# Putting the y stage of an attention and two-layer feed-forward kernel into the planner's one order

## The chip, the cores and the metric

The kernel runs on one core of a Trainium2 chip. The metric is device time in microseconds (us) of one execution, as the median of several runs. The engines are TensorE (PE), VectorE (DVE), ScalarE (ACT), GpSimd (POOL) and SyncE (SP, which issues most DMAs). Each works through its own list of instructions in order.

## The reference

Three layers follow each other; the second uses x = attention output (2304 tokens, 512 wide), the third uses y.

```python
# attention: B=4, H=8, S=576, D=64, causal softmax, plus a memory read-out, mixed by sigmoid(beta)
x = (g * mem_out + (1 - g) * local)          # -> [2304, 512]
# layer 2: w_in [512, 2048], w_out [2048, 512]
r = np.maximum(x @ w_in, 0.0)
y = (s * (r * r) + b) @ w_out
# layer 3: w_gate, w_val [512, 1536], w_out2 [1536, 512]
out = (1 / (1 + np.exp(-(y @ w_gate))) * (y @ w_val)) @ w_out2
```

## The kernel before, in words

Every large product is taken in two terms: an operand is split into a rounded high part and the low rest, and PE adds hi times hi, lo times hi and hi times lo. So each product step is 12 matmuls: 3 terms by 4 blocks of 128.

**Attention** works on 16 jobs, each two heads of one batch. When the four jobs of a batch are done, their sum XB is split into x (`s_hi` on ACT, L885; `s_lo`, L889, on the engine that `ENG["split"]` names, here DVE), in two windows of 256 and 320 tokens. **h** takes 128 chunks, 8 such windows by 16 blocks `f` of w_in (L316); ACT applies the relu (L326), and SP stores pairs of chunks to the scratch tensor `r_d` (L330). **The y stage** goes over 5 windows of tokens (256, then four of 512) by 16 blocks f, 80 steps in all; I call them y0 to y4. A step loads r back (`load_r`, L977), squares it on ACT (L1030), scales and shifts it on DVE (L1031), rounds the high part gh on ACT (L1035), takes the low part gl on DVE in even steps and on POOL in odd ones (L1037), and runs 12 matmuls with the block of w_out (L1053). After a window, `y_out` splits the sums on ACT and DVE (L1007) and stores the first three windows (L1013). **The gv stage** (L1124, L1094) then does layer 3.

**Weights** lie in memory as 64-bit words. `load_weight` (L219) loads a block of 512 KB into a raw buffer of the pool `stage` (two buffers; L228, L232), then scales on ACT (L242), shifts and joins on DVE (L245, L248, L254), rounds the high part on ACT (L260) and takes the low part on POOL (L263), which releases the raw buffer.

**The order.** `Plan` (L36) is a list scheduler: each task has an engine, a cost in ns, an urgency (the smaller, the sooner), what it reads, and slots that it needs; `plan.order()` gives one order for all engines, and the program is issued in it under `tc.manual_schedule()` (L958). `TUNE` holds the urgencies. Only the attention, the w_in loads and h are in the plan. The y stage stands behind it (from `att.close()`, L961), written as a plain loop with `load_gv` at every third step; there the framework's scheduler decides. Pools that reuse attention memory open when the last instruction on that memory is done.

```python
    with tc.manual_schedule():
        for n in plan.order():
            plan.tasks[n][2]()
    att.close()
```

Of the kernel before, what the change touches and what calls it, by code (L numbers as in the profile page):

```python
# [20 lines left out]
FB = 1  # L21
RATE = 160.0

TUNE = {
# [3 lines left out]
    "relu": -5000.0,  # L28
}
ENG = {"split": "DVE"}  # L30
RR = 4
LEAD = 1
DEFER = 3
# [112 lines left out]
def attention_moe_kernel(  # L146
# [72 lines left out]
    def load_weight(pool, src, name, cols, pieces=None):  # L219
# [204 lines left out]
    def stack_lo(t, ds):  # L424
# [9 lines left out]
        "PTC": 1, "XB": 1, "x0": 1, f"x{SPLIT}": 1, "raw": 2, "f": FB, "w": 1, "wt": 16,  # L434
# [14 lines left out]
    def plan_load(j):  # L449
# [454 lines left out]

    def plan_h(m):
        b, c0, n, f = chunks[m]
        u = AT["h"] + m * AT["hs"]
        add(
# [15 lines left out]

    def plan_w_in(f):
        u = AT["w"] + f * AT["ws"]

        def pieces(load, scaled, rest, joined, high, low):
            def last():
                w_in_sb[f] = low()  # L930

            add("SP", 600, load, u + AT["lw"], new=[("raw", ("raw", f)), ("wt", ("wt", f))], late=1900, size=5e5)
            add("ACT", 670, scaled, u, reads=[("raw", f)], new=[("f", ("f", f))])
            add("DVE", 1400, rest, u, writes=[("raw", f)])
            add("DVE", 800, joined, u, reads=[("f", f)], writes=[("raw", f)])
            add("ACT", 660, high, u, reads=[("raw", f)], writes=[("wt", f)])
            add("POOL", 1360, last, u, reads=[("raw", f)], writes=[("wt", f)])

        load_weight(w1, w_in[:, f * P : (f + 1) * P], f"w_in{f}", True, pieces)
# [21 lines left out]
    att.close()  # L961


    w2 = ctx.enter_context(tc.tile_pool(name="w2", bufs=19, side="right"))
    wins = [(max(0, i), 512 + min(i, 0)) for i in range(-NT % 512 and NT % 512 - 512, NT, 512)]
    w_out_sb = {}
    gp = ExitStack()
    gpool = gp.enter_context(tc.tile_pool(name="gp", bufs=2, side="right"))
    steps = [(wi, f) for wi in range(len(wins)) for f in range(NF)]
    r_sb = {}  # L970

    def load_r(n):
# [22 lines left out]
    ps_yb = gp.enter_context(tc.tile_pool(name="ps_yb", bufs=4, space=PSUM))
    ybuf = {}
    kept = 2
    ngv = 0
    ydone = []

    def y_out():
        wi, acc = ydone.pop()
        c0, n = wins[wi]
        yt = yp.tile([P, 2, NK, 512], F32R, tag="y", name=f"ya{wi}")
        for d in range(NK):
            nc.scalar.copy(yt[:, 0, d, :n], acc[d][:, :n])
            nc.vector.tensor_tensor(  # L1007
                out=yt[:, 1, d, :n], in0=acc[d][:, :n], in1=yt[:, 0, d, :n].bitcast(F32),
                op=ALU.subtract,
            )  # L1010
        if wi < len(wins) - kept:
            for x, dst in enumerate((yh_d, yl_d)):
                nc.sync.dma_start(  # L1013
                    dst[:, c0 : c0 + n].rearrange("(c p) n -> p c n", p=P),
                    yt[:, x, :, :n].bitcast(F32),
                )
        else:
# [166 lines left out]
```

## Time and profile before

| what | us |
|---|---|
| median of 3 runs | 1155.8 (1155.66 to 1156.09) |
| the profiled execution | 1153.03 |
| its span, first to last instruction | 1151.0 |
| busy in the span: PE / DVE / ACT / POOL | 1082.7 / 601.5 / 541.1 / 332.5 |

The mean clock granted to TensorE is 0.98 of full speed. The profiled execution is 2.8 us under the median of the runs, and 2.0 us of it lie outside the span. Read the profile by stage: attention with h to some 472 us, y to 699 us, gv to the end; each has another limit.

### The profile page before, as it was taken

Reading aid. Unit: us, or ns where it says so; the run is one execution under the profiler, and the core shown is the slowest. Engines: PE = TensorE matmul, PEld = TensorE weight load, DVE = VectorE, ACT = ScalarE, POOL = GpSimd, SP = SyncE. Lnnn points to the kernel's source line nnn. Section 1 sums busy time; section 2 is a strip of 40 time slices with the busy share of each in tenths; the row PEclk is TensorE's granted clock in tenths of the full one; section 3 lists DMA queues with packets and bytes.
Section 4 is the critical chain, followed back from the end, with each engine's and each line's share of the span. In section 5 each row is a group of like instructions: output and inputs, shape, how many; then the busy total and the mean of one; then the engine's idle time right before and its main releaser. Section 6 shows DMA issues by size and latency. Waiting matters only on the chain.

```text
span 1151.0 us, 16974 instructions
## 1 busy us (share of the span) xinstructions
PE 1082.7 (94%) x6232; PEld 932.8 (81%) x6232; DVE 601.5 (52%) x1178; ACT 541.1 (47%) x1176; POOL 332.5 (29%) x363
## 2 busy tenths in 40 slices
PE   4787999999999998998899989999999999999998
PEld 3665998999999998876678867888888888888897
DVE  5988879776766745688864587311211111111122
ACT  5768877777777754566545555211111111111121
POOL 5646656443354223444432353000000000000000
PEclk9778999999999999999999999999999999999999
DMA  5333454332322157676645454002000200100000
GB/s 118 90 92 83 137 147 133 95 104 83 86 81 74 47 164 208 198 225 192 219 141 180 133 169 120 9 0 73 37 1 7 104 1 1 37 37 1 1 38 19
DMA packets 128290, 105.96 MB, mean 92 GB/s; under 512 B 67024, under 2 KB 110032, under 8 KB 128208
## 3 DMA queue, kind: packets, MB, share of 16 engines
q1 hardware_dynamic: 125616, 100.17, 29.4%
q10 hardware_dynamic: 2592, 4.72, 1.1%
q8 instruction: 49, 0.80, 0.3%
q14 instruction: 33, 0.27, 0.1%
HBM read 76.03 MB, written 28.84 MB: 91 GB/s over the span
## 4 chain that ended last, share of the span: by engine, by line
PE 71%; DVE 10%; DMA 8%; POOL 4%; ACT 3%; issue 3%; SPq 0%; DVEq 0%; POOLq 0%; ACTq 0%
PE gv L1124 25%; PE oa L1094 13%; PE h L316 12%; PE y L1053 7%; DMA raw_w_out<-in_moe_w_out_dram 4%; PE sc L620 3%; PE acc L800 2%; PE acc L801 2%; DMA raw_gv<-in_moe_w_val_dram 2%; POOL P L678 2%; PE pt_B L747 2%; DMA raw_gv<-in_moe_w_gate_dram 1%; POOL w_out L263 1%; PE sc L646 1%; PE acc L804 1%
## 5 line engine op out<-in xcount | busy, mean ns | idle before, releaser
L316 PE MATMUL h<-x,w_in 128*128 128x256 f32 (+1 forms) x1536 | 230.4, 302 | 6.7 <-ACT r L326 5.6
L316 PEld LDWEIGHTS h<-x,w_in 128*128 128x128 f32 x1536 | 208.8, 190 | 16.0 <-ACT r L326 9.9
L1133 DVE TENSOR_TENSOR sg<-gv,sg 128x512 f32<-128x512 f32 (+1 forms) x60 | 38.2, 637 | 300.5 <-PE gv L1124 300.5
L1124 PE MATMUL gv<-yb,gv 128*128 128x512 f32 (+1 forms) x864 | 172.4, 355 | 0.0
L1053 PE MATMUL y<-gh,w_out 128*128 128x512 f32 (+1 forms) x640 | 148.8, 375 | 17.3 <-ACT gh L1035 17.2
L1124 PEld LDWEIGHTS gv<-yb,gv 128*128 128x128 f32 x864 | 143.9, 188 | 25.2
L1053 PEld LDWEIGHTS y<-gh,w_out 128*128 128x128 f32 x640 | 112.0, 189 | 44.7 <-ACT gh L1035 25.1
L1094 PE MATMUL oa<-w_out,ph 128*128 128x512 f32 x432 | 143.7, 392 | 0.0
L1124 PE MATMUL gv<-ya,gv 128*128 128x512 f32 x576 | 136.2, 392 | 0.1
L1124 PEld LDWEIGHTS gv<-ya,gv 128*128 128x128 f32 x576 | 108.0, 188 | 24.6 <-ACT sg L1131 0.5
L1131 ACT ACTIVATE sg<-gv 128x512 f32<-128x512 f32 (+1 forms) x60 | 33.3, 555 | 195.6 <-PE gv L1124 195.4
L1135 ACT CAST ph<-sg 128x512 fp32r<-128x512 f32 (+1 forms) x60 | 34.6, 577 | 146.4 <-DVE sg L1133 146.4
L678 POOL TENSOR_SCALAR P<-P,rs 128x384 f32<-128x384 f32 (+4 forms) x144 | 86.3, 623 | 41.2 <-DVE rs L674 32.9
L1094 PEld LDWEIGHTS oa<-w_out,ph 128*128 128x128 f32 x432 | 81.1, 188 | 17.8
L662 ACT ACTIVATE P<-P,nm 128x384 f32<-128x384 f32 (+2 forms) x144 | 83.7, 583 | 13.4 <-DVE nm L600 12.3
L1094 PE MATMUL oa<-w_out,pl 128*128 128x512 f32 x216 | 84.5, 391 | 0.0
L600 DVE CUSTOM_DVE_ANT_0 P<-sc,mask 128x384 f32<-128x384 f32 (+2 forms) x144 | 70.3, 514 | 24.2 <-PE sc L620 14.9
L1053 PE MATMUL y<-gl,w_out 128*128 128x512 f32 (+1 forms) x320 | 80.3, 373 | 2.5 <-POOL gl L1037 1.5
L1031 DVE TENSOR_SCALAR rr<-rr,sb_s,sb_b 128x512 f32<-128x512 f32 (+1 forms) x80 | 55.2, 697 | 45.7 <-ACT rr L1030 45.4
L1037 POOL TENSOR_TENSOR gl<-rr,gh 128x512 fp32r<-128x512 f32 (+1 forms) x40 | 52.4, 1309 | 76.3 <-ACT gh L1035 60.4
L326 ACT ACTIVATE r<-h 128x320 f32<-128x320 f32 (+1 forms) x128 | 52.4, 409 | 45.3 <-PE h L316 38.5
L1030 ACT ACTIVATE rr<-rr 128x512 f32<-128x512 f32 (+1 forms) x80 | 46.6, 588 | 51.2 <-DMA rr<-relu_scratch 50.7
(118 smaller groups left out, 1648.5 us busy)
## 6 DMA issues: line engine op xcount, KB each, us to landing
rr<-relu_scratch SPq DMA_DIRECT2D x64, 256.0 KB, 3.1
raw_w_out<-in_moe_w_out_dram SPq DMA_DIRECT2D x28, 512.0 KB, 3.6
relu_scratch<-r SPq DMA_DIRECT2D x32, 320.0 KB, 2.2
raw_w_in<-in_moe_w_in_dram SPq DMA_DIRECT2D x16, 512.0 KB, 4.1
relu_scratch<-r SPq DMA_DIRECT2D x32, 256.0 KB, 2.5
raw_gv<-in_moe_w_gate_dram SPq DMA_DIRECT2D x12, 512.0 KB, 3.7
raw_gv<-in_moe_w_val_dram SPq DMA_DIRECT2D x12, 512.0 KB, 3.8
out_dram<-o ACTq DMA_DIRECT2D x18, 256.0 KB, 2.0
```

The costliest lines, as they stand in the source:

```text
L316: nc.tensor.matmul(t[:, :n], wt[:, wi, c], x[:, xi, c], start=(m == 0), stop=(m == 3 * NK - 1))
L326: nc.scalar.activation(rts[b, c0, f - f % 2][:, f % 2, :n], t[:, :n], AF.Relu)
L600: nc.vector.tensor_tensor_reduce(out=pr, in0=ps, in1=mk, scale=1.0, scalar=3e38, op0=ALU.add, op1=ALU.min, accum_out=nm,)
L662: nc.scalar.activation(pr, pr, AF.Exp, bias=T.pop(("nm", j, e, t)), scale=-1.0, accum_out=T["sums", j][:, col : col + 1],)
L678: nc.gpsimd.tensor_scalar(out=pr, in0=pr, scalar1=T["rs", j, part][:, n : n + 1], scalar2=1.0, op0=ALU.mult, op1=ALU.mult,)
L1030: nc.scalar.activation(r, r, AF.Square)
L1031: nc.vector.tensor_scalar(out=r, in0=r, scalar1=sb_s, scalar2=sb_b, op0=ALU.mult, op1=ALU.add)
L1037: (nc.vector, nc.gpsimd)[step % 2].tensor_tensor(out=gl, in0=r, in1=gh.bitcast(F32), op=ALU.subtract)
L1053: nc.tensor.matmul(acc[d][:, :n], w_out_sb[f][:, x, d], y, start=(f == 0 and x == 0 and y is gh), stop=(f == NF - 1 and y is gl),)
L1094: nc.tensor.matmul(acc[tt], a[:, ts], w_out2_sb[f][:, x].rearrange("p c f -> p (c f)"), start=(f == 0 and a is ph and x == 0), stop=(f == ...
L1124: nc.tensor.matmul(t[:, :n], wt[:, a, c], yt[:, x, c, :n], start=(m == 0), stop=(m == 3 * NK - 1),)
L1133: nc.vector.tensor_tensor(out=pf[:, :n], in0=ps[1][:, :n], in1=sg[:, :n], op=ALU.mult)
```

## The change

- All tasks of the y stage enter the plan: the 16 w_out blocks (`plan_w_out`), the first 16 of the 24 w_gate and w_val blocks (`plan_gv`), the steps (`plan_step`) and the window ends (`plan_y_out`). Two tasks of no engine open the pools: `open_y`, when all attention tasks are issued ("bar1"), and `open_yp`, when all h tasks are too ("bar2"). y0 needs only the first, so its steps may stand between the last h chunks; y1 to y4 need the second.
- The late weights get raw buffers of their own, three instead of two ("raw2"). The pool w2 has 16 buffers instead of 19, so three of the twelve w_out2 blocks more wait for the end of the y stage (w3 has 4 instead of 1).
- `ENG["split"]` goes from DVE to POOL.
- y is stored by block d, 8 DMAs of up to 256 KB in a window, instead of 2 of up to 1 MB.
- The planner's costs, its DMA rate and every number in `TUNE` are set anew, so the attention's order moves too. The last 8 blocks of w_gate and w_val, all of w_out2 and the gv stage stay outside the plan.

```diff
-RATE = 160.0
+RATE = 250.0
...
-    "relu": -5000.0,
+    "relu": -5000.0, "wo": 29802.5, "wos": 17.7, "gv": 39611.4, "gvs": 94.4, "y": 13878.2,
+    "lead": -44.8, "lr": -193.8, "ys": -70.4, "yss": -0.0,
 }
-ENG = {"split": "DVE"}
+ENG = {"split": "POOL"}
 RR = 4
-LEAD = 1
-DEFER = 3
...
+        "raw2": 3, "f2": FB, "w2": 16, "rr": RR, "gh": 3, "gl": 3, "yacc": 2, "yt": 2,
...
+    def plan_weight(pool, src, name, cols, u, key, tag, done, ins=(), late=False):
+        raw = "raw2" if late else "raw"
...
+            add(
+                "SP", 450, load, u + AT["lw"], reads=ins,
+                new=[(raw, ("raw", key)), (tag, key)], late=1900, size=5e5,
+            )
+            f = "f2" if late else "f"
+            add("ACT", 670, scaled, u, reads=[("raw", key)], new=[(f, ("f", key))])
+            add("DVE", 1500, rest, u, writes=[("raw", key)])
+            add("DVE", 850, joined, u, reads=[("f", key)], writes=[("raw", key)])
+            add("ACT", 660, high, u, reads=[("raw", key)], writes=[key])
+            add("POOL", 1360, last, u, reads=[("raw", key)], writes=[key])
...
+    def open_y():
+        att.close()
+        Y["w2"] = ctx.enter_context(tc.tile_pool(name="w2", bufs=16, side="right"))
+        Y["gp"] = gp.enter_context(tc.tile_pool(name="gp", bufs=2, side="right"))
+        Y["stage"] = gp.enter_context(tc.tile_pool(name="stage2", bufs=3, side="right"))
+        Y["ps", 0] = gp.enter_context(tc.tile_pool(name="ps_ya", bufs=4, space=PSUM, side="right"))
...
+        add(
+            "PE", 12 * mm(n), y_mm, u,
+            reads=[gk, ("gl", step), ("wo", f)] + (["bar2"] if wi else ["bar1"])
+            + ([("yc", step - 1)] if step else []),
+            writes=[("yc", step)] + ([] if new else [("ya", wi)]), new=new, late=250,
+        )
...
+        def store(d):
+            nc.sync.dma_start(yh_d[d * P : (d + 1) * P, c0 : c0 + n], box["t"][:, 0, d, :n].bitcast(F32))
+            nc.sync.dma_start(yl_d[d * P : (d + 1) * P, c0 : c0 + n], box["t"][:, 1, d, :n].bitcast(F32))
...
+    for key, opened, before in (("bar1", open_y, bar1), ("bar2", open_yp, h_parts)):
+        n = add("BAR", 0, opened, 0, reads=["bar1"] if key == "bar2" else [], writes=[key], late=0)
+        plan.tasks[n][4].update(before)
...
-    w2 = ctx.enter_context(tc.tile_pool(name="w2", bufs=19, side="right"))
...
-            if ngv < 19 and f % 3 == 0:
-                load_gv(ngv)
-                ngv += 1
...
+        for f in range(8)
     ]
     gp.close()
-    w3 = ctx.enter_context(tc.tile_pool(name="w3", bufs=1, side="right"))
+    w3 = ctx.enter_context(tc.tile_pool(name="w3", bufs=NF2 - 8, side="right"))
```

Three places show how instructions move. In the names, h_3_256_12 is the chunk of batch 3, window from token 256, block f = 12; y0_2 is the sum of window y0 in output block 2; gh0_1, gl0_1 and rr0_1 are window 0, step 1; gv3_1 is block 3 of w_val (gv3_0: of w_gate). x12 counts alike matmuls.

**PE, where h ends and y0 starts.** Before:

```order
L316 MATMUL h_3_256_12_6187<-x3_256_5777,w_in12_2050 128x320 x12
L316 MATMUL h_3_256_13_6203<-x3_256_5777,w_in13_2193 128x320 x12
L316 MATMUL h_3_256_14_6217<-x3_256_5777,w_in14_2434 128x320 x12
L316 MATMUL h_3_256_15_6233<-x3_256_5777,w_in15_2512 128x320 x12
L1053 MATMUL y0_0_6443<-gh0_0_6439,w_out0_6261 128x256
L1053 MATMUL y0_1_6444<-gh0_0_6439,w_out0_6261 128x256
```

With the change, from the last matmuls of the first y0 step on:

```order
L1044 MATMUL y0_2_5973<-gl0_0_5896,w_out0_5849 128x256
L1044 MATMUL y0_3_5974<-gl0_0_5896,w_out0_5849 128x256
L315 MATMUL h_3_0_9_5993<-x3_0_5730,w_in9_1680 128x256 x12
L315 MATMUL h_3_0_10_6018<-x3_0_5730,w_in10_1817 128x256 x12
L315 MATMUL h_3_0_11_6040<-x3_0_5730,w_in11_1892 128x256 x12
L1044 MATMUL y0_0_5971<-gh0_1_5894,w_out1_5866 128x256
L1044 MATMUL y0_1_5972<-gh0_1_5894,w_out1_5866 128x256
```

Before, all h stands ahead of the first y0 step. Now that step stands behind chunk 8 of the next to last window, with 23 h chunks to come; 14 of the 16 y0 steps stand ahead of the last of these, and two behind it.

**DVE in window y1**, the scaling of steps 6 to 9 and what lies between. Before:

```order
L1031 TENSOR_SCALAR rr1_6_6881<-rr1_6_6881,sb_s_71,sb_b_72 128x512
L248 SCALAR_TENSOR_TENSOR raw_gv3_1_6933<-raw_gv3_1_6933 128x512
L1031 TENSOR_SCALAR rr1_7_6901<-rr1_7_6901,sb_s_71,sb_b_72 128x512
L254 SCALAR_TENSOR_TENSOR raw_gv3_1_6933<-f_gv3_1_6935,raw_gv3_1_6933 128x512
L1037 TENSOR_TENSOR gl1_6_6968<-rr1_6_6881,gh1_6_6966 128x512
L1031 TENSOR_SCALAR rr1_8_6942<-rr1_8_6942,sb_s_71,sb_b_72 128x512
L1031 TENSOR_SCALAR rr1_9_6962<-rr1_9_6962,sb_s_71,sb_b_72 128x512
```

With the change:

```order
L1019 TENSOR_SCALAR rr1_6_6823<-rr1_6_6823,sb_s_71,sb_b_72 128x512
L253 SCALAR_TENSOR_TENSOR raw_gv0_1_6742<-f_gv0_1_6825,raw_gv0_1_6742 128x512
L1030 TENSOR_TENSOR gl1_4_6888<-rr1_4_6722,gh1_4_6883 128x512
L244 TENSOR_SCALAR raw_gv1_0_6773<-raw_gv1_0_6773 128x512
L247 SCALAR_TENSOR_TENSOR raw_gv1_0_6773<-raw_gv1_0_6773 128x512
L253 SCALAR_TENSOR_TENSOR raw_gv1_0_6773<-f_gv1_0_6886,raw_gv1_0_6773 128x512
L244 TENSOR_SCALAR raw_gv1_1_6836<-raw_gv1_1_6836 128x512
L247 SCALAR_TENSOR_TENSOR raw_gv1_1_6836<-raw_gv1_1_6836 128x512
L1030 TENSOR_TENSOR gl1_6_6941<-rr1_6_6823,gh1_6_6935 128x512
L1019 TENSOR_SCALAR rr1_7_6869<-rr1_7_6869,sb_s_71,sb_b_72 128x512
L1019 TENSOR_SCALAR rr1_8_6892<-rr1_8_6892,sb_s_71,sb_b_72 128x512
L253 SCALAR_TENSOR_TENSOR raw_gv1_1_6836<-f_gv1_1_6915,raw_gv1_1_6836 128x512
```

In both orders a block of w_gate or w_val takes three DVE instructions among the scalings and low parts. Before, 16 such blocks stand between the scalings of step 0 of y1 and step 12 of y2, in 28 steps; now 16 stand between those of step 3 of y1 and step 1 of y3, in 30 steps.

**The first split of x**, batch 0, tokens 0 to 255. On DVE before, around it:

```order
L600 ISA P5_0_2_1387,nm5_2_1388<-sc5_0_2_1371,mask_88 128x384
L600 ISA nm5_2_1388 128x1
L889 TENSOR_TENSOR x0_0_1346<-XB0_361,x0_0_1346 128x1024
L670 SCALAR_TENSOR_TENSOR rs4_0_1405<-sums4_1118,iom_93 128x5
L674 RECIPROCAL rs4_0_1405<-rs4_0_1405 128x5
L889 TENSOR_TENSOR x0_256_1365<-XB0_361,x0_256_1365 128x1280
```

On POOL with the change:

```order
L262 TENSOR_TENSOR w_in3_686<-raw_w_in3_687,w_in3_686 128x512
L262 TENSOR_TENSOR w_in4_947<-raw_w_in4_948,w_in4_947 128x512
L527 TENSOR_TENSOR phit4_1243<-phi4_1122,zbc4_954 128x640
L889 TENSOR_TENSOR x0_0_1271<-XB0_410,x0_0_1271 128x1024
L584 TENSOR_SCALAR VHL5_1321<-rawv_92 128x10x64
L587 TENSOR_TENSOR VHL5_1321<-rawv_92,VHL5_1321 128x10x64
```

The low part of x leaves DVE for POOL, behind two weights and a phi product. The addition into XB that completes these tokens is DVE's instruction 206 before and 200 now, and the first h matmul is PE's number 480 before and 458 now; it now stands before the transposes and scores of the next job, which stood ahead of it.

## Rows read from the trace of the kernel before

**Rows 1.** Busy us by stretch: PE, PEld, DVE, ACT, POOL; clock, DMA, GB/s.

```profile
0.00:114.00 114.00, 79.61 (x481) 64.40 (x481) 91.60 (x231) 79.33 (x189) 68.95 (x92) 0.84 0.39 96
114.00:120.00 6.00, 4.70 (x37) 4.36 (x36) 5.29 (x11) 4.50 (x11) 4.85 (x7) 1.00 0.43 136
120.00:400.00 280.00, 277.13 (x2211) 263.08 (x2209) 208.68 (x513) 210.56 (x524) 135.38 (x173) 0.99 0.34 99
```

**Rows 2.** The same view: h tail, y0, y1-y2, y3 on, last steps, gv.

```profile
405.47:471.62 66.15, 60.16 (x423) 56.89 (x423) 32.48 (x50) 34.51 (x74) 19.02 (x15) 1.00 0.64 194
471.62:501.36 29.74, 25.09 (x194) 23.49 (x192) 22.95 (x38) 17.73 (x40) 14.34 (x14) 1.00 0.66 202
501.36:604.34 102.98, 92.06 (x384) 70.77 (x385) 82.02 (x106) 57.93 (x103) 44.03 (x31) 1.00 0.61 190
604.34:664.18 59.84, 59.84 (x265) 49.55 (x264) 29.78 (x45) 32.78 (x59) 18.74 (x14) 1.00 0.50 152
664.18:699.04 34.86, 30.60 (x122) 23.23 (x120) 28.30 (x36) 17.55 (x31) 17.87 (x13) 0.95 0.53 166
699.04:1147.00 447.96, 447.88 (x2089) 371.62 (x2087) 98.20 (x151) 83.00 (x145) 9.34 (x7) 1.00 0.08 28
```

**Rows 3.** Timeline of PE at the first h: start, us, [idle before <-releaser].

```profile
111.55 0.74 PE L413 MATMUL ft<-ident,phi 128*128 128x128 f32 x5 [1.44 <-DVE QT L478]
...
114.80 0.97 PE L316 MATMUL h<-x,w_in 128*128 128x256 f32 x6 [0.66 <-DVE x L889]
```

**Rows 4.** Timeline of DVE: an addition into batch 0's x, and the last split.

```profile
104.38 0.42 DVE L828 TENSOR_TENSOR XB<-acc,XB 64x256 f32<-64x256 f32 x1 [0.17 <-ACT XB L824]
...
412.64 1.49 DVE L889 TENSOR_TENSOR x<-XB,x 128x1280 fp32r<-128x1280 f32 x1 [5.92 <-ACT x L885]
```

**Rows 5.** Groups by line and shape, POOL: busy us, mean ns | idle before.

```profile
L587 POOL TENSOR_TENSOR VHL<-rawv,VHL 128x640 fp32r<-128x640 f32 x16 | 26.6, 1661 | 1.3
```

**Rows 6.** Timeline of PE: two h chunks of 320 columns, and what follows.

```profile
400.47 3.77 PE L316 MATMUL h<-x,w_in 128*128 128x320 f32 x24
404.08 0.31 PE L800 MATMUL acc<-PTB,VHL 128*128 128x320 f32 x1
```

**Rows 7.** What PE waited for, 404 to 503 us: total, times, longest.

```profile
PE h L316 <- ACT r L326: 5.6, 8, 2.7
```

**Rows 8.** Timeline of SP: first and last of 11 w_out loads; gv loads.

```profile
429.17 0.33 SPq L232 DMA_DIRECT2D raw_w_out<-in_moe_w_out_dram  x1
...
470.77 0.35 SPq L232 DMA_DIRECT2D raw_w_out<-in_moe_w_out_dram  x1
...
502.20 0.38 SPq L228 DMA_DIRECT2D raw_gv<-in_moe_w_gate_dram  x1
...
526.88 0.38 SPq L228 DMA_DIRECT2D raw_gv<-in_moe_w_gate_dram  x1
```

**Rows 9.** The page's part 6: KB of one DMA, us to landing.

```profile
raw_w_out<-in_moe_w_out_dram SPq DMA_DIRECT2D x28, 512.0 KB, 3.6
```

**Rows 10.** Groups by line and shape, DVE, 400 to 700 us.

```profile
L1031 DVE TENSOR_SCALAR rr<-rr,sb_s,sb_b 128x512 f32<-128x512 f32 x64 | 47.4, 744 | 41.7 <-ACT rr L1030 41.3
L1037 DVE TENSOR_TENSOR gl<-rr,gh 128x512 fp32r<-128x512 f32 x32 | 26.4, 826 | 1.6 <-ACT gh L1035 1.6
L248 DVE SCALAR_TENSOR_TENSOR raw_gv<-raw_gv 128x512 int32<-128x512 int32 x24 | 21.2, 882 | 0.6
L245 DVE TENSOR_SCALAR raw_gv<-raw_gv 128x512 int32<-128x512 int32 x24 | 20.9, 870 | 11.4 <-DMA raw_gv<-in_moe_w_gate_dram 6.1 <-DMA raw_gv<-in_moe_w_val_dram 5.0
L254 DVE SCALAR_TENSOR_TENSOR raw_gv<-f_gv,raw_gv 128x512 int32<-128x512 int32 x24 | 20.5, 854 | 1.1
```

**Rows 11.** Timeline of DVE, then of POOL, around one overlap.

```profile
504.58 0.54 DVE L1031 TENSOR_SCALAR rr<-rr,sb_s,sb_b 128x512 f32<-128x512 f32 x1
...
507.51 1.63 DVE L1031 TENSOR_SCALAR rr<-rr,sb_s,sb_b 128x512 f32<-128x512 f32 x1
...
507.54 1.32 POOL L263 TENSOR_TENSOR gv<-raw_gv,gv 128x512 fp32r<-128x512 f32 x1 [3.67 <-ACT gv L260]
```

More of the change, by code (lines that the diff above doesn't have):

```diff
@@ L925, in plan_w_in @@
-    def plan_w_in(f):
-        u = AT["w"] + f * AT["ws"]
+            h_parts.append(add(
+                "SP", 450, lambda: h_store(b, c0, n, f), v, reads=[("r", m - 1)],
+                writes=[("stored", b, c0, f // 2)], late=2500, size=n * 1024,
+            ))
+    def plan_weight(pool, src, name, cols, u, key, tag, done, ins=(), late=False):
+        raw = "raw2" if late else "raw"
         def pieces(load, scaled, rest, joined, high, low):
             def last():
[L930 to L939, printed above, removed]
+                done(low())
+            add(
[8 more added lines that the diff above has]
+            add("POOL", 1360, last, u, reads=[("raw", key)], writes=[key])
+        load_weight(pool, src, name, cols, pieces, Late("stage") if late else stage)
@@ new lines, in attention_moe_kernel @@
+    NW = len(wins)
+    steps = [(wi, f) for wi in range(NW) for f in range(NF)]
+    kept = 2
+    NGV = 16
+    gp = ExitStack()
+    def open_y():
[4 more added lines that the diff above has]
+        Y["ps", 0] = gp.enter_context(tc.tile_pool(name="ps_ya", bufs=4, space=PSUM, side="right"))
@@ new lines, in plan_y_out, with hi, lo @@
+    def plan_y_out(wi, u):
+        c0, n = wins[wi]
+        box = {}
+        def hi(d):
+            if d == 0:
+                box["t"] = Y["yp"].tile([P, 2, NK, 512], F32R, tag="y", name=f"ya{wi}")
+                if wi >= NW - kept:
+                    ybuf[wi] = box["t"]
+            nc.scalar.copy(box["t"][:, 0, d, :n], accs[wi][d][:, :n])
+        def lo(d):
+            yt = box["t"]
+            nc.vector.tensor_tensor(
+                out=yt[:, 1, d, :n], in0=accs[wi][d][:, :n], in1=yt[:, 0, d, :n].bitcast(F32),
+                op=ALU.subtract,
+            )
+        def store(d):
+            nc.sync.dma_start(yh_d[d * P : (d + 1) * P, c0 : c0 + n], box["t"][:, 0, d, :n].bitcast(F32))
+            nc.sync.dma_start(yl_d[d * P : (d + 1) * P, c0 : c0 + n], box["t"][:, 1, d, :n].bitcast(F32))
+        v = u - 5
+        for d in range(NK):
+            add(
+                "ACT", act(n), lambda d=d: hi(d), v,
+                reads=[("ya", wi), "bar2"] + ([("yt", wi)] if d else []), writes=[("yp", wi, d)],
+                new=[] if d else [("yt", ("yt", wi))],
+            )
+            add("DVE", dve(n), lambda d=d: lo(d), v, reads=[("ya", wi)], writes=[("yp", wi, d)])
+        if wi < NW - kept:
+            for d in range(NK):
+                add(
+                    "SP", 900, lambda d=d: store(d), u + AT["ys"] + d * AT["yss"],
+                    reads=[("yt", wi), ("yp", wi, d)], late=2500, size=n * 1024,
+                )
@@ L953, in attention_moe_kernel @@
         plan_products(j)
+    bar1 = list(range(len(plan.tasks)))
     for m in range(len(chunks)):
         plan_h(m)
+    for key, opened, before in (("bar1", open_y, bar1), ("bar2", open_yp, h_parts)):
+        n = add("BAR", 0, opened, 0, reads=["bar1"] if key == "bar2" else [], writes=[key], late=0)
+        plan.tasks[n][4].update(before)
+    for f in range(NF):
+        plan_w_out(f)
+    for step in range(len(steps)):
+        plan_step(step)
+    for n in range(NGV):
+        plan_gv(n)
     load_consts()
@@ L995, in attention_moe_kernel @@
[L995 to L1017, printed above, removed]
-            ybuf[wi] = yt
@@ L1075, in attention_moe_kernel @@
+    w_out2_sb += [
+        load_weight(w3, w_out2[f * P : (f + 1) * P], f"w_out2_{f}", False) for f in range(8, NF2)
+    ]
     op = ctx.enter_context(tc.tile_pool(name="op", bufs=2, side="right"))
```

183 lines of the change are left out of this document (103 added, 80 removed), and 6 rows, old and new, of the table TUNE.

## The prediction

> **What bounds the kernel now.** I read the time by stretches first, since a share over the whole span mixes stages with different limits. Until 114 us PE is busy 79.6 us and DVE 91.6 [rows 1]: the attention of the first batch waits for its vector work, and no h is there yet to fill PE. From 120 to 400 us PE is busy 277.13 of 280 us. Behind the attention, at 405.47 us, five stretches follow [rows 2]: the last 35 h chunks, y0, y1 with y2, the 22 steps of y3 and the start of y4, and the last ten steps. Only the fourth is without gaps: 59.84 us for 22 steps, 2.72 us a step. From 699.04 us on, the gv stage keeps PE busy 447.88 of 447.96 us. So there is something to gain in three places only: before 120 us, between 405 and 604 us, and in the last ten y steps.
>
> How much? A 320-column h chunk takes (404.08 - 400.47) / 2 = 1.80 us where nothing stops it [rows 6]; 256 columns take in proportion 1.44. The 35 chunks are 19 wide and 16 narrow ones, 57.2 us, and y0 has 16 steps of 1.44, 23.0 us. Together 80.3 us; they took 66.15 + 29.74 = 95.9, so 15.6 are lost. y1 and y2, 32 steps, need 87.0 and took 102.98: 15.9 lost. The last ten steps need 27.2 and took 34.86: 7.7 lost. In all 39.2 us.
>
> **The part before 120 us.** The addition that completes the first 256 tokens of x comes at 104.38 us [rows 4], yet the first full run of h starts at 114.80 [rows 3]: the split and the next job's transposes and scores stand between. PE lost 1.44 us and 0.66 us there to DVE, and 1.3 of the 6 us after 114 [rows 1]. In the new order h comes directly behind the job's last products, 22 matmuls sooner. The split now runs on POOL. No row shows 1024 columns there; the nearest is two-input work on 640 columns, 1.66 us [rows 5], so I estimate 2.66 for 1024 and 3.32 for 1280 columns by proportion. ACT rounds the high part first, at the rate of the DVE split of 1280 columns (1.49 us, [rows 4]) about 1.2. Then x can be ready at 104.8 + 1.2 + 2.7 = 108.7 us, before PE ran dry at 111.55 - 1.44 = 110.1. So the 1.44 and 1.3 us can be filled: 2.7 us. The addition also stands six instructions earlier on DVE; at 208.68 / 513 = 0.41 us each [rows 1] that is 2.4 us more, 5.1 in all. Against it, eight splits of 3 us on average burden POOL, which is already busy 68.95 of 114 us. I take **3.5 us gained**; the ends are 5.1 gained and 1.7 lost (x late by one more POOL instruction of that length). Between 120 and 405 us PE has 2.9 us to lose or win: nothing.
>
> **h tail and y0.** The y pools open when the last split is done. It started at 412.64 and took 1.49 us on DVE [rows 4]; 3.32 on POOL open them 1.8 us later, at about 415.9. Four r loads are issued first, some 0.35 us each [rows 8], then w_out0, which lands 3.6 us later [rows 9]: 420.9. Three DVE passes (0.87 + 0.88 + 0.85, [rows 10]), one on ACT of about 0.9 and one on POOL of about 1.33 (1.66 x 512 / 640) make it ready at 425.7. PE reaches the first y0 step after three wide and nine narrow chunks, 18.4 us, at 423.9: a first wait of about 2 us. Then 14 steps stand among 23 chunks, 7 x 1.44 + 16 x 1.80 + 14 x 1.44 = 59.1 us, one step per 4.2 us, and each wants a new block of w_out. Before, ten intervals between w_out loads took 470.77 - 429.17 = 41.6 us, 4.16 each [rows 8], with two raw buffers; now there are three. So the supply just suffices. What else stops PE there is the relu: 5.6 us of h waits end on ACT [rows 7]. The new order places ACT's weight passes and relus together, and DVE has room (32.48 of 66.15 us busy [rows 2]), so I keep 30% of the old loss, 4.6 us, by choice. New loss 6.6 instead of 15.6: **9 us gained**. The ends are 13.6 (only the first wait) and nothing.
>
> **y1 and y2.** Here DVE is the engine to watch: 82.02 of 102.98 us busy [rows 2]. Before, 16 weight blocks fall in 28 steps: 16 x 2.606 + 28 x 0.744 + 14 x 0.826 [rows 10] + 8 window ends at about 0.83 = 80.7 us of DVE, in 28 x 2.72 + 15.9 = 92.1 us: 88% used. Now the 16 blocks are spread over 30 steps: 41.7 + 22.3 + 12.4 + 6.6 = 83.0 us against 81.6 of PE. At the same 88% that takes 94.3 us, a loss of 12.7; if DVE never stood idle, 83.0, a loss of 1.4. A third raw buffer and the order worked out with DVE's costs should lift the use; I take 92%, 90.2 us, a loss of 8.6: **7 us gained**, ends 14.5 and nothing (85% gives 97.6, a loss of 16).
>
> **The rest.** The last ten steps still share DVE with six weight blocks, as before: no gain; the ends are 4 us either way, half of the loss. In front of the gv stage 12 blocks of w_out2 remain instead of 9; three more are 8 us of DVE, 3 x 2.606, beside a PE that is covered by gv products for 72 matmuls: **1 us lost**, ends 0 and 3. The y stores in pieces add 18 issues of 0.35 us on SP, 6 us, on no path that PE waits for: nothing, unless loads of r queue behind them.
>
> **Sum.** -3.5 - 9 - 7 + 0 + 1 = -18.5 us. Against the profiled execution, 1153.03, that is 1134.5; its own time stands 2.8 us under the median, so the median goes from 1155.8 to about **1137 us**.
>
> **A rule that speaks against it.** While POOL took a weight's low part from 507.54 to 508.86 us, a scaling on DVE that takes 0.54 us alone took 1.63 [rows 11]. POOL got none of its work taken away here, and gets the splits on top. If the two stay in each other's way, DVE's use in y1 and y2 remains 88%.
>
> The Trainium skill, page "SBUF — State Buffer", section "SBUF: two separate sides", states why such a thing would happen: the port pair that DVE and GpSimd share is locked by one instruction for its whole length, and the other waits. By that rule, the trace agrees (0.54 against 1.63 us), and the first rival below would be the outcome.
>
> **Rivals.**
>
> *Contention stays.* 3 us gained in y1 and y2 (15.9 - 12.7), none before 120 us, half of the 9 in the h tail, 1 lost: -6.5, about 1149. For it: the pair of durations above, and that no DVE or POOL work is removed. Against it: the blocks are more spread. Chance 0.2, 1144 to 1153.
>
> *Slower: PE's single line of h and y0.* PE now has h chunks queued behind y0 steps. If w_out blocks come slower than one per 4.2 us, h, which never waited for them, waits too. Beside the work of y1 the gv loads came at (526.88 - 502.20) / 4 = 6.2 us [rows 8]. At 6.2 PE would lose 2 + 14 x (6.2 - 4.2) = 30 us in place of 15.6, 14.4 more; the other terms give 9.5 back: 5 slower, 1161. It decides from an interval of about 6 us on. Against it: y0 has half the columns per step, and the 4.16 us was measured just there. Chance 0.11.
>
> *The attention pays.* Eight splits, 24 us of POOL, stand ahead of probability tiles that PE needs. If each makes PE wait 2 us, 16 of the 18.5 are lost: 1153 to 1158. PE had no such gap between 120 and 400 us. Chance 0.06.
>
> *Nearly all gaps go.* The order is then right enough to win the 39.2 us but for the first wait and half of the last steps, with 3.5 in front: 39.2 - 2 - 3.9 + 3.5 = 36.8, 1119; from 1129 down I count it here. Chance 0.13.
>
> That the plan does not take hold I leave out: the instruction lists above show the new order on PE, DVE and POOL.
>
> **Numbers.** The forecast holds 0.5, from 1129 to 1144. Differences under 0.2%, 2.3 us, cannot be told from no change by a measurement of this kernel: faster means under 1153.5. Faster gets 0.5 + 0.2 + 0.13 and a little of the attention rival, 0.84; slower 0.11; the same 0.05. The range from 1122 to 1153 leaves out some 0.05 below and 0.15 above.
>
> **What would show it.** Right: the first h before 111 us; the stretch from the end of the attention to the first y1 step some 87 us instead of 95.9; y1 and y2 near 96 us with DVE busier than 85%; w_out loads at most 4.3 us apart. Wrong: PE waits for h on POOL's split; waits of y0 steps on POOL's w_out pass, with gaps over 6 us between loads; y1 and y2 still over 100 us; new gaps between 120 and 400 us.

## The result, and the profile after

The changed kernel takes **1128.28 us** (median of 4 runs, 1125.16 to 1132.56) against 1155.94 of the kernel before, timed beside it: the ratio is 0.976, its 95% interval 0.973 to 0.980. Its profiled execution took 1132.56 us, with a span of 1130.6 us, 20.4 less than before. It is the slowest of the four; a second trace of the same kernel, below, has a span of 1122.9. The forecast was 1137 with a range of 1122 to 1153.

Busy time by stretch, of the kernel after, with the columns of [rows 1] and the stretches of [rows 2]: the h tail with y0, y1 and y2, y3 and six steps of y4, the last ten steps, gv.

```profile
0.00:114.00 114.00, 84.15 (x509) 68.27 (x510) 94.03 (x229) 80.66 (x190) 72.27 (x93) 0.82 0.38 94
114.00:120.00 6.00, 6.00 (x51) 5.69 (x50) 5.83 (x16) 5.74 (x15) 5.59 (x8) 1.00 0.50 137
120.00:400.00 280.00, 274.49 (x2196) 260.38 (x2194) 209.87 (x505) 208.79 (x522) 145.69 (x178) 1.00 0.35 101
...
401.77:492.05 90.28, 83.05 (x614) 82.02 (x613) 55.09 (x81) 50.72 (x112) 36.35 (x27) 0.96 0.64 202
492.05:584.74 92.69, 89.33 (x386) 72.95 (x385) 78.11 (x101) 55.48 (x101) 46.16 (x32) 0.98 0.64 202
584.74:644.58 59.84, 59.84 (x265) 49.56 (x264) 32.49 (x47) 33.65 (x59) 20.06 (x15) 1.00 0.50 152
644.58:678.49 33.91, 30.05 (x122) 23.32 (x120) 27.36 (x33) 17.17 (x29) 16.04 (x12) 0.95 0.55 167
678.49:1126.00 447.51, 447.18 (x2086) 371.24 (x2085) 104.18 (x159) 87.21 (x152) 13.23 (x10) 1.00 0.09 31
```

Read each stretch against its pair in [rows 2]. The pure h stretch starts at 401.77 instead of 405.47 us: 3.7 won. The h tail with y0 takes 90.28 us against 66.15 + 29.74: 5.6 won. y1 and y2 take 92.69 against 102.98: 10.3 won. The middle runs without gaps at the same 59.84. The last ten steps take 33.91 against 34.86: 1.0 won. The gv stage and the end take what they took, 452.1 against 452.0. Together 20.4.

Before 120 us PE is busy 90.15 us, 5.84 more than in [rows 1], and between 120 and 400 us 2.64 less. What the start wins is thus partly given back in the attention's middle, where the kernel before had hardly any gaps.

In the h tail one wait stands out. Timeline of PE in the kernel after, around 420 us (start, us, what, and the idle time before it with what ended it):

```profile
416.35 3.21 PE L315 MATMUL h<-x,w_in 128*128 128x256 f32 x24 [0.51 <-ACT r L325]
424.53 2.93 PE L315 MATMUL h<-x,w_in 128*128 128x256 f32 x12 [4.97 <-ACT r L325]
```

The timeline of ACT in the same place:

```profile
421.53 0.69 ACT L241 ACTIVATE f_w_out<-raw_w_out 128x512 f32<-128x512 f32 x1 [3.16 <-DMA raw_w_out<-in_moe_w_out_dram]
423.52 0.68 ACT L259 CAST w_out<-raw_w_out 128x512 fp32r<-128x512 f32 x1 [1.30 <-DVE raw_w_out L253]
424.09 0.38 ACT L325 ACTIVATE r<-h 128x256 f32<-128x256 f32 x1
```

And from the chain of waits the load that it goes back to:

```profile
414.08 7.43 DMA raw_w_out<-in_moe_w_out_dram
```

PE waits 4.97 us for a relu. ACT has that relu ready to do, but its list holds the scaling and the rounding of w_out0 ahead of it, and w_out0 landed 7.43 us after its issue, not the 3.6 of [rows 9]. Three weights, seven r tiles and two stores of r were issued between 411.89 and 419.57 us; that this crowd alone makes w_out0 late is not shown, as the next trace says. And after the wait the same twelve matmuls of an h chunk take 2.93 us instead of about 1.6: the granted clock fell.

### The profile page after: what moved, and what is told of

Read it like the earlier page. It is cut to its first block, busy times and chain, and to the rows that moved or that the text cites. A ratio compares the mean times of both kernels' runs of the same rounds, so it can differ in the third digit from the quotient of the medians.

```text
span 1130.6 us, 16983 instructions
## 1 busy us (share of the span) xinstructions
PE 1076.8 (95%) x6232; PEld 935.6 (83%) x6232; DVE 608.2 (54%) x1170; ACT 540.4 (48%) x1176; POOL 355.4 (31%) x371
## 4 chain that ended last, share of the span: by engine, by line
PE 73%; DVE 8%; DMA 6%; POOL 4%; issue 4%; ACT 4%; SPq 0%; DVEq 0%; POOLq 0%; ACTq 0%
PE gv L1206 25%; PE oa L1176 13%; PE h L315 13%; PE y L1044 7%; PE sc L620 3%; PE acc L800 2%; PE acc L801 2%; DMA rr<-relu_scratch 2%; PE pt_B L747 1%; DMA raw_gv<-in_moe_w_gate_dram 1%; DMA raw_w_out<-in_moe_w_out_dram 1%; PE sc L646 1%; POOL P L678 1%; PE acc L804 1%; POOL gv L262 1%
## 5 line engine op out<-in xcount | busy, mean ns | idle before, releaser
L1044 PEld LDWEIGHTS y<-gh,w_out 128*128 128x128 f32 x640 | 114.3, 191 | 31.6 <-ACT gh L1025 9.0
L1019 DVE TENSOR_SCALAR rr<-rr,sb_s,sb_b 128x512 f32<-128x512 f32 (+1 forms) x80 | 52.4, 662 | 57.1 <-ACT rr L1015 43.6
```

The costliest lines, as they stand in the source:

```text
L1019: nc.vector.tensor_scalar(out=r, in0=r, scalar1=sb_s, scalar2=sb_b, op0=ALU.mult, op1=ALU.add)
L1044: nc.tensor.matmul(accs[wi][d][:, :n], w_out_sb[f][:, x, d], y, start=(f == 0 and x == 0 and y is gh), stop=(f == NF - 1 and y is gl),)
```

## The experiments

All are compared through the kernel before, which is timed beside them; the changed kernel's median is 1128.3 and, in its second timing, 1127.2 us, a ratio of 0.977 (0.975 to 0.979). The intervals of four variants overlap with that one: y0 behind h, two raw buffers, the whole stores, the late first loads. Their times alone don't set them apart from the changed kernel; what is said of them rests on their traces.

**The changed kernel again.** No edit.

> The changed kernel, unaltered, for its spread and a second trace. In its first trace PE waits 4.97 us for a relu at 419.6 us (ACT stands at the scaling of w_out0, whose load landed late), and the granted clock falls to 0.83 in the 20 us after. Theory: the spread of its four runs, 1125.2 to 1132.6 us, comes from the clock after such a wait. Then this run is near 1128 us, and its trace shows the wait again, with or without the fall; where the fall is absent, the stretch from the end of the attention to y1 is about 2.5 us shorter than 90.3. Rival: the spread comes from elsewhere; then that stretch is the same and another one differs.

Measured: 1127.22 us, ratio 0.977 (0.975 to 0.979). Two stretches of this trace, and the 20 us after the wait, in this trace and then in the first:

```profile
401.33:486.49 85.16, 80.85 (x614) 79.60 (x614) 54.87 (x81) 50.85 (x112) 36.57 (x27) 1.00 0.67 214
486.49:576.62 90.13, 87.92 (x386) 71.86 (x385) 79.21 (x101) 55.83 (x101) 44.61 (x32) 1.00 0.66 208
420.00:440.00 20.00, 18.35 (x152) 18.35 (x153) 14.43 (x23) 12.76 (x30) 8.33 (x7) 1.00 0.73 236
```

```profile
420.00:440.00 20.00, 15.47 (x109) 15.47 (x110) 11.83 (x20) 10.04 (x23) 6.01 (x6) 0.83 0.57 191
```

The load of w_out0, from the chain of waits of this trace:

```profile
414.22 4.41 DMA raw_w_out<-in_moe_w_out_dram
```

The wait is there again, this time 2.5 us long, since w_out0 landed after 4.41 us with the same issues around it; and the clock stays at 1.00 behind it. The stretch is 5.1 us shorter: 2.4 by the shorter wait, and the rest I put down to the clock. Another 2.6 come from y1 and y2. So the kernel's spread of 7 us starts in a few waits of PE whose length varies and after which the clock falls or doesn't. Two traces show this; they don't show what decides it.

**y0 behind h.**

```diff
-            reads=[gk, ("gl", step), ("wo", f)] + (["bar2"] if wi else ["bar1"])
+            reads=[gk, ("gl", step), ("wo", f)] + ["bar1", "bar2"]
```

> One part of the change undone: y0 steps, like the others, wait for all h chunks; weights, order numbers and buffers stay. Theory (standing y0 among the h chunks is what won 5.6 us between the attention and y1): the stretch returns to about 96 us and the time rises by 4 to 8 us. Rival A (the new order of loads and ACT work won it; the interleaving is beside the point): within 2 us of the changed kernel. Rival B (the interleaving costs: PE in one line with the w_out blocks, the 5 us wait): 3 to 6 us faster.

Measured: 1131.85 us, ratio 0.980 (0.977 to 0.983): about 4 us slower than the changed kernel by the medians. The h tail with y0:

```profile
401.37:494.95 93.58, 85.39 (x613) 83.99 (x613) 56.57 (x83) 50.84 (x111) 39.46 (x28) 0.95 0.64 201
```

The relu wait is as long as in the changed kernel's first trace, 5.25 us, and the stretch 3.3 us longer than that trace's 90.28. So the interleaving itself is worth some 3 to 4 us, by one trace and by medians whose intervals overlap. The theory's return to 96 is half there: with y0 behind h the new order still gains on the 95.9 of before. That PE's single line of h and y0 costs time is not seen.

**Two raw buffers.**

```diff
-        "raw2": 3, "f2": FB, ...
+        "raw2": 2, "f2": FB, ...
-        Y["stage"] = gp.enter_context(tc.tile_pool(name="stage2", bufs=3, side="right"))
+        Y["stage"] = gp.enter_context(tc.tile_pool(name="stage2", bufs=2, side="right"))
```

> The late weights get two raw buffers instead of three, in the pool and in the planner's slots; the rest is as changed. Theory (the third buffer lets a load run while two blocks are converted, and so gives most of the 10.3 us won in y1 and y2): 5 to 12 us slower than the changed kernel, with y1 and y2 near 100 us and w_out loads over 4.3 us apart. Rival (the order did it, not the buffer): within 2 us.

Measured: 1131.01 us, ratio 0.980 (0.977 to 0.983): some 3 us slower by the medians. h tail with y0, then y1 and y2:

```profile
397.75:492.94 95.19, 85.80 (x613) 83.68 (x613) 55.44 (x82) 52.11 (x113) 34.74 (x27) 0.93 0.60 192
492.94:582.02 89.08, 89.08 (x385) 73.56 (x385) 76.19 (x97) 55.29 (x99) 42.41 (x30) 0.98 0.67 210
```

The theory put the buffer's worth in the wrong place. In y1 and y2 two buffers are enough: PE has no gap at all, 89.08 us. In y0 they are not: from the fourth to the last the w_out loads come every 4.7 us (4.45 and 4.22 in the two traces of the changed kernel), y0 steps wait 6.0 us for w_out, and the clock is 0.66 from 480 to 500 us, over the end of the stretch. So what y1 and y2 won does not need the third buffer; the order that the planner made, here for two, is enough.

**The attention's part alone.** The kernel before with the new `TUNE` (its y entries have nothing to act on there) and:

```diff
-RATE = 160.0
+RATE = 250.0
-ENG = {"split": "DVE"}
+ENG = {"split": "POOL"}
```

as well as the planner's new costs of loads, stores and weight passes.

> One part of the change alone: the kernel before with the new numbers for attention, w_in and h, the planner's new costs and the split of x on POOL; its y stage stays the loop of before, in the framework's order. PE's order up to the last h chunks is that of the changed kernel. Theory (the attention's part is what the trace shows at the start of the pure h stretch, 405.5 before and 401.5 now): 3 to 6 us faster than before, with that point at 401 to 402 us and y1 and y2 still near 103 us. Rival (the new order of the attention helps only through what it leaves for the y stage): within 2 us of before.

Measured: 1148.09 us, ratio 0.995 (0.993 to 0.997): 5.7 us faster than before. h tail with y0, then y1 and y2:

```profile
397.74:492.72 94.98, 85.98 (x613) 80.43 (x612) 52.62 (x85) 53.29 (x115) 38.77 (x31) 1.00 0.63 199
492.72:596.93 104.21, 92.90 (x385) 72.06 (x385) 83.34 (x107) 58.94 (x105) 44.30 (x32) 0.98 0.60 192
```

The theory holds in the size: the attention's part is worth 4 to 8 us by the interval, and the y stage behind it is what it was, 95.0 and 104.2 us. The rest of the gain, some 20 us, is the y stage in the plan. The pure h stretch starts at 397.74, 4 us sooner than expected and than in the changed kernel, with the same order up to there on PE; the last section comes back to that. The mean clock of this kernel's seven runs is 0.980 to 0.991, that of the changed kernel's nine 0.976 to 0.986. So the 5.7 us can hold some of a clock that no edit explains, and the y stage's share is 20 us or somewhat more.

**The split of x back on DVE.**

```diff
-ENG = {"split": "POOL"}
+ENG = {"split": "DVE"}
```

> One number of the change undone: x's low part goes back to DVE, the planner works with that, all else as changed. Theory (POOL's splits cost something by opening the y pools later, 2.96 against 1.49 us, but free DVE in the start): the first h comes at 104 to 108 us, the first y0 load some 1.5 us sooner, and the time is within 3 us of the changed kernel's 1127.8. Rival (the split on POOL is what lets h start 10 us sooner): 4 us slower or more, first h after 108 us.

Measured: 1136.68 us, ratio 0.987 (0.984 to 0.989): some 9 us slower than the changed kernel by the medians, 11 by the ratios. The first h, in the timeline of PE:

```profile
102.84 3.11 PE L315 MATMUL h<-x,w_in 128*128 128x256 f32 x24
```

The attention's middle, busy time by stretch:

```profile
120.00:400.00 280.00, 271.26 (x2122) 255.34 (x2121) 206.44 (x509) 206.37 (x517) 141.74 (x177) 0.97 0.34 97
```

The theory misses, and the rival has the time without the reason. The first h comes as early as with POOL (103.60), so it does not need POOL. Part of the loss is in the middle: 3.2 us less PE work between 120 and 400 us than with POOL, at a clock of 0.97 instead of 1.00, and the pure h stretch starts at 404.79. The rest lies behind it. The theory had the y loads some 1.5 us sooner; but the last split starts at 419.01 instead of 408.9 us, and the first w_out load is issued at 423.61 instead of 414.08. The other numbers were set for POOL, so what the engine and what the numbers cost is not told apart; with these numbers the engine is not a free choice.

**The y stores whole.** In the planner, too, they are one task, which needs all four blocks of the window.

```diff
-            nc.sync.dma_start(yh_d[d * P : (d + 1) * P, c0 : c0 + n], ...)
-            nc.sync.dma_start(yl_d[d * P : (d + 1) * P, c0 : c0 + n], ...)
+            for x, dst in enumerate((yh_d, yl_d)):
+                nc.sync.dma_start(
+                    dst[:, c0 : c0 + n].rearrange("(c p) n -> p c n", p=P),
+                    box["t"][:, x, :, :n].bitcast(F32),
+                )
```

> One part of the change undone: each y window is stored by two DMAs of up to 1 MB again instead of eight of up to 256 KB; the rest is as changed. Theory (the stores in pieces are in nobody's way): within 2 us of the changed kernel's 1127.8. Rival A (the r loads of the next window queue on SP behind the eight stores, and the two waits of 1 to 2 us after the end of y1 come from that): those waits go, 2 to 4 us faster. Rival B (larger stores hold the r loads up longer): 2 to 5 us slower, with longer waits there.

Measured: 1129.47 us, ratio 0.980 (0.978 to 0.982): 1 to 2 us slower than the changed kernel by the medians, some 4 by the ratios. The h tail with y0, and y1 with y2:

```profile
400.81:488.76 87.95, 82.81 (x614) 81.12 (x613) 55.33 (x81) 50.75 (x112) 36.40 (x27) 0.98 0.65 208
488.76:583.29 94.53, 89.07 (x386) 71.53 (x385) 78.03 (x102) 56.19 (x102) 45.40 (x33) 1.00 0.64 201
```

The h tail lies between the two traces of the changed kernel. y1 and y2 do not: 94.53 us against 92.69 and 90.13, with five waits of PE, 5.4 us in all, instead of two. These waits end on ACT and DVE. ACT waits less for r than in the changed kernel, 6.4 us against 17.5 and 11.4, so rival B's reason is not the one. Rival A is refuted, the stores in pieces cost nothing that shows; whether whole ones cost 2 to 4 us is open.

**The planner told that the first loads land late.**

```diff
-                new=[(raw, ("raw", key)), (tag, key)], late=1900, size=5e5,
+                new=[(raw, ("raw", key)), (tag, key)],
+                late=7000 if key in (("wo", 0), ("wo", 1), ("wo", 2)) else 1900, size=5e5,
```

> The planner is told that the first three w_out loads land 7 us after issue instead of 1.9; the kernel's instructions are the same, only the order behind the attention moves: the relus of two h chunks now stand ahead of the scaling of w_out0 on ACT. Theory (that relu behind a late load made PE wait 5 us, and the wait brought the clock down): the wait shrinks to under 1 us, the clock stays at 1.00 from 420 to 440 us, and the time falls by 4 to 7 us. Rival (PE would soon wait for w_out0 anyway): the wait moves to the first y0 step, and the time is within 2 us.

Measured: 1131.11 us, ratio 0.980 (0.978 to 0.982): no faster, if anything 3 us slower. Timeline of ACT:

```profile
416.88 0.66 ACT L325 ACTIVATE r<-h 128x256 f32<-128x256 f32 x2 [3.33 <-DMA relu_scratch<-r]
417.42 0.67 ACT L241 ACTIVATE f_w_out<-raw_w_out 128x512 f32<-128x512 f32 x1
```

The relu now stands ahead of w_out0's scaling, and waits all the same: for the store that must empty its buffer, which lands late among the same transfers. PE waits 2.6 us. The theory named one instruction that stands behind a late transfer; with that one out of the way, another does.

**22 weight blocks in the plan.**

```diff
-    NGV = 16
+    NGV = 22
...
+    def GVINS(n):
+        return ["bar1"]
...
-            w1, src, name, True, AT["gv"] + n * AT["gvs"], ("gv", n), "wt",
-            lambda t: gv.__setitem__(divmod(n, 2), t), ins=["bar1"], late=True,
+            w1 if n < 16 else Late("w2"), src, name, True, AT["gv"] + n * AT["gvs"], ("gv", n),
+            "wt" if n < 16 else "w2", lambda t: gv.__setitem__(divmod(n, 2), t), ins=GVINS(n), late=True,
```

> The next step of the change: 22 of the 24 w_gate and w_val blocks are in the plan instead of 16, the six new ones in the buffers that w_out leaves, with three raw buffers; they still fall into the last window. Theory (in the last ten steps, 33.9 us where 27.2 would do, the six blocks stand in an order that the planner did not choose): the stretch from step 6 of y4 to the gv stage falls to 29 to 31 us, 3 to 5 us faster than the changed kernel. Rival (DVE and POOL have no time for six blocks and the steps there, whoever orders them): that stretch stays over 33 us and the time within 2 us.

Measured: 1120.48 us, ratio 0.971 (0.969 to 0.974): some 7 us faster than the changed kernel. The last ten steps:

```profile
641.75:668.96 27.21, 27.21 (x121) 22.52 (x120) 18.92 (x21) 12.60 (x23) 16.49 (x12) 1.00 0.36 113
```

27.21 us, without a gap; the theory hoped for 29 to 31. But the window also holds less work: DVE is busy 18.92 us in it, against 27.36 in the changed kernel. Of the 27.36, 7.57 us were passes of three w_out2 blocks, in a view of the raw w_out tiles alone (the changed kernel, then this one; DVE, ACT, POOL):

```profile
644.58:678.49 33.91, 7.57 (x9) 3.59 (x6) 2.75 (x2) 0.95 0.55 167
641.75:668.96 27.21, 0.00 (x0) 0.00 (x0) 0.00 (x0) 1.00 0.36 113
```

Here w_out2 comes behind the window, and the gv stage and the end take no longer for it, 451.6 us against 452.1. So neither theory nor rival has it: part of the work left the window, and what the order and the third raw buffer of the six blocks did for the rest is not told apart. I had taken that work as bound to the window.

**The blocks spread over y1 to y3.**

```diff
+    def GVINS(n):
+        return ["bar1", ("yc", min(13 + 3 * n, 66))]
...
-            "wt" if n < 16 else "w2", ..., ins=["bar1"], late=True,
+            "wt" if n < 16 else "w2", ..., ins=GVINS(n), late=True,
```

> As gv22, and each of the first 16 blocks of w_gate and w_val may be loaded only when PE has done step 13 + 3n, so that they lie over 47 steps, y1 to y3, instead of the 30 before. Theory (two or three waits that are left in y1 and y2, 3.4 us with the clock at 0.92 in one 20 us stretch, come from steps where two blocks press together on DVE): y1 to the middle of y4 runs at 2.72 us a step, 3 to 6 us faster than gv22 with a narrower spread. Rival (those waits come from r loads queued behind other DMAs, not from DVE): waits of the same size stay at the window ends, and the time is within 2 us of gv22.

Measured: **1116.57 us** (1113.69 to 1117.89), ratio 0.968 (0.966 to 0.970): the fastest of all, some 11 us under the changed kernel and 37 under the one before.

```profile
488.59:575.66 87.07, 87.07 (x386) 72.10 (x385) 62.08 (x89) 53.75 (x94) 37.47 (x28) 1.00 0.64 200
575.66:635.50 59.84, 59.84 (x265) 49.57 (x264) 44.86 (x64) 37.17 (x67) 23.40 (x18) 1.00 0.64 201
635.50:662.71 27.21, 27.21 (x121) 22.53 (x120) 19.19 (x21) 13.01 (x23) 16.79 (x12) 1.00 0.36 112
```

All 64 steps of y1 to y4 run without a gap, 174.12 us where 64 x 2.72 = 174.1 is what PE needs. DVE has 62 us of work in y1 and y2 instead of the changed kernel's 78, and 45 instead of 32 in the next stretch, which had room. The theory holds in that the waits are gone, and they are gone in the next run too, which has the same spread. What it is worth is less than it looks. These are, for the 22 blocks of the run before, the h tail with y0 and then y1 with y2; and for the spread ones the h tail with y0:

```profile
401.60:492.87 91.27, 83.13 (x614) 81.59 (x613) 54.34 (x82) 51.28 (x112) 38.22 (x27) 0.98 0.63 201
492.87:581.91 89.04, 88.54 (x385) 72.85 (x385) 78.20 (x100) 55.34 (x100) 44.42 (x31) 0.99 0.66 209
401.88:488.59 86.71, 82.13 (x613) 81.06 (x613) 54.31 (x80) 50.89 (x112) 36.45 (x27) 0.98 0.64 205
```

Without the spread, one wait of 0.5 us was left there in this trace; with two raw buffers and no spread there was none. Of the 5.6 us between these two traces, y1 and y2 give 2.0, and the h tail with y0 gives 4.6, where PE waits 4.5 us in all instead of 8.2.

**The first loads set apart.** On top of the last one:

```diff
+    WAIT = {1: 100, 2: 102}
...
+            ins=["bar1"] + ([("hc", WAIT[f])] if f in WAIT else []), late=True,
...
+                late=4500 if key in (("wo", 0), ("wo", 1), ("wo", 2)) else 1900, size=5e5,
```

> As gv22_spread, and the loads of w_out1 and w_out2 may be issued only after h chunks 100 and 102 (of 128), and the planner counts 4.5 us for the first three to land. Theory (three weights and seven r tiles asked for within some 5 us make each other land late, w_out0 after 5 to 7 us, and either w_out0's scaling or a relu's buffer then holds ACT and PE): w_out0 lands within 4.5 us, no PE wait for a relu over 1 us at 415 to 425 us, the clock stays 1.00 from 420 to 440 us, and the time falls 2 to 5 us under gv22_spread. Rival (the burst is not it; ACT is held by whatever comes next): a wait of 2 to 3 us remains there and the time is within 1.5 us of gv22_spread.

Measured: 1122.4 us, ratio 0.973 (0.972 to 0.975): 6 us slower than without. Timeline of ACT, at the relu that waits:

```profile
420.09 0.66 ACT L325 ACTIVATE r<-h 128x256 f32<-128x256 f32 x2 [2.63 <-DMA relu_scratch<-r]
```

And of PE, at the end of y0, with the h tail and y0 as a whole:

```profile
486.29 0.74 PE L1051 MATMUL y<-gh,w_out 128*128 128x256 f32 x4 [1.10 <-ACT w_out L259]
...
490.49 1.22 PE L1051 MATMUL y<-gh,w_out 128*128 128x256 f32 x4 [1.07 <-ACT w_out L259]
...
400.88:494.37 93.49, 84.72 (x613) 82.57 (x613) 56.87 (x82) 50.84 (x113) 35.76 (x27) 0.96 0.64 193
```

In effect the third load alone moved, to 418.48 us; the second is still issued 0.95 us after the first. The first still takes 5.5 us to land, the relu waits for its buffer again, and PE for the relu, 1.9 us. The 6 us are lost behind that: the stretch takes 93.49 us instead of 86.71, and its steps wait 6.4 us for w_out instead of 1.3. So the theory is not borne out; but with one load moved the burst is hardly thinned, and how the wait at 420 us could go stays open.

## Why the prediction was right, and where it was too small

The direction, the place and the range were right, and two thirds of the size: 18.5 us forecast, 20.4 in the trace and 26 to 28 between the medians. The median, 1128.3, lies just over the edge of the likeliest case (1129 to 1144), towards the rival in which nearly all gaps go, and by the prediction's own count, from 1129 down, inside it. In the first trace the terms err both ways: 3.4 us too much in the h tail, 3.3 too little in y1 and y2. That 18.5 stands so near to 20.4 is in part luck. And one of its signs of being wrong came true: there are new gaps between 120 and 400 us.

**The part before 120 us** (3.5): the pure h stretch starts 3.7 us sooner, and this part alone gives 5.7 us. The way there is as said, the first h comes sooner, by 10 us even, at 103.60 instead of 113.64: the addition that completes x comes 6.1 us sooner, not 2.4, and x is ready at 104.1, not 108.7. Two more steps were off. "Between 120 and 405 us nothing" is not so: 2.64 us of what the start wins are lost there. And POOL's split, priced at 2.66 and 3.32 us, takes 2.42 and 2.96 us.

**h tail and y0** (9): 5.6 us in the first trace, 10.7 in the second. The price of the interleaving's supply was about right: w_out every 4.45 and 4.22 us, and y0 waits 1.7 and 1.3 us for it in all. What failed is the first wait: 2 us, at the first y0 step, from the median landing time of a load. The load took 7.43 us in the first trace and 4.41 in the second, and its wait reached PE earlier, through a relu queued on ACT behind the load's scaling: 4.97 and 2.53 us. I had costed who waits for w_out0, and not what is queued behind the engine that waits.

**y1 and y2** (7): 10.3 and 12.9 us. This is the term that was mis-sized. I took DVE's work over DVE's use for the time: 83.0 us in 30 steps, at 92% instead of 88%. Here are the 28 steps of before and the 30 of the two traces after:

```profile
501.36:593.46 92.10, 81.19 (x336) 61.76 (x337) 77.73 (x100) 53.45 (x95) 41.45 (x29) 1.00 0.64 203
500.24:587.46 87.22, 83.86 (x361) 68.44 (x360) 71.37 (x90) 52.62 (x94) 43.96 (x30) 0.98 0.61 196
494.67:579.34 84.67, 82.46 (x361) 67.35 (x360) 72.38 (x90) 52.58 (x93) 42.57 (x30) 1.00 0.63 201
```

DVE's use is 84% before and 82 and 85% after: it did not rise. DVE's work in PE's time of these steps is 71 to 72 us, not 83; two of the 16 blocks and half of the window ends that I counted are done outside it, and instructions that I added up overlap at their ends. So DVE's use is not what sets the time. From 520 to 540 us DVE is busy 19.64 and 19.90 of 20 us, while PE has no gap; in the next 20 us it is busy 15.71 and 16.55, and there PE loses 3.4 and 1.4 us. The full stretch in the second trace:

```profile
520.00:540.00 20.00, 20.00 (x89) 16.55 (x89) 19.90 (x27) 13.87 (x26) 9.82 (x7) 1.00 0.73 229
```

And two scalings of the same shape in it, in the timeline of DVE, with POOL's instruction beside the first:

```profile
520.52 1.53 DVE L1019 TENSOR_SCALAR rr<-rr,sb_s,sb_b 128x512 f32<-128x512 f32 x1
...
524.75 0.54 DVE L1019 TENSOR_SCALAR rr<-rr,sb_s,sb_b 128x512 f32<-128x512 f32 x1
...
520.40 1.36 POOL L1030 TENSOR_TENSOR gl<-rr,gh 128x512 fp32r<-128x512 f32 x1 [2.48 <-ACT gh L1025]
```

So an engine can be full without anyone waiting for it, and have room while PE waits. The reason that I gave, a third raw buffer, is wrong in this place, as the run with two shows.

**The rivals.** *Contention stays* falls in its result and not in its fact: in the rows above, of the second trace, one scaling takes 1.53 us beside POOL's instruction and another 0.54 with POOL idle, as in [rows 11]. The Trainium skill, page "SBUF — State Buffer", section "SBUF: two separate sides", says that DVE and GpSimd lock each other out of a shared port pair. By that rule, the trace agrees. Yet y1 and y2 lose 3.1 us in that trace instead of 12.7: the new order hides most of it. *PE's single line* finds no support in its own experiment: without it the stretch is 3.3 us longer, not shorter. *The attention pays*: 2.64 us are lost instead of 16, and hardly for its reason, since PE's waits there that end on POOL's tiles are 0.9 us in all, and with the splits on DVE the middle lost more. *Nearly all gaps go* was not the change, and is what the spread version does for y1 to y4.

**The rest** (0 and 1 lost): 1.0 won and 0.1 lost in the first trace. But "no gain in the last ten steps", because DVE shares them with six blocks, took the blocks as bound to that place; with 22 blocks in the plan w_out2 leaves it, and the loss is gone.

## What to carry to other kernels

A busy share tells how much work an engine has, not what it costs: in y1 and y2 DVE was busy 80% with 10.9 us of gaps on PE before, and with two raw buffers and the planner's order 86% without any. So when a stage loses time on an engine that is not full, look at its order before its work. In an in-order queue the price of a late transfer is paid by whatever stands behind the instruction that waits for it, so follow that queue, not only the user of the data. And what lies outside a good planner's reach is the next place to look: the last six blocks of w_gate and w_val in the plan, and the first 16 better spread, were worth some 11 us more.

## What the runs showed of the hardware that was not expected

PE waits of 2 to 5 us are followed in some executions by a lower granted clock and in others not. From 420 to 440 us it was 0.83 after the wait of 4.97 us and after the 5.25 of y0 behind h, 0.91 after waits of 3.95, 2.84, 2.33 and 1.89 us (22 blocks, spread, whole stores, loads apart), and 1.00 after 2.53 and 2.58 us (the second trace, late first loads). So the length of the wait alone does not decide it. Of the two levels, 1.2 and 2.4 GHz, 0.83 means the first for about a third of that stretch. The clock at the start varies too, with the attention's order the same. Until 114 us it was 0.82 in the changed kernel (the first row above) and 0.93 in the run with two raw buffers:

```profile
0.00:114.00 114.00, 79.84 (x532) 63.78 (x532) 95.93 (x237) 82.36 (x197) 76.11 (x97) 0.93 0.39 99
```

With 0.93, which the attention's part alone and the late first loads had too, the pure h stretch begins at 397.75 us, in the changed kernel at 401.33 and 401.77, 4 us that no edit there explains; what decides it stays open. And w_out0, a load of 512 KB, one that lands in 3.7 us by the median, took 4.41, 4.48, 4.66, 5.76, 7.43 and 7.69 us in six traces that issue the same loads and stores around it (the changed kernel twice, whole stores, spread, 22 blocks, y0 behind h). A crowd of transfers is there each time; what makes the difference is not shown.
